# The last output stores of an attention and gated-unit kernel, on other issuing engines

## The chip, the cores and the metric

The kernel runs on one core of one Trainium2 chip. The metric is device time in microseconds. The kernel before takes 338.45 us, the median of 3 runs (337.93 to 338.51). The profiled execution took 338.22 us, of which the span from its first to its last instruction is 336.1 us.

Engines are named as in the profile: PE is TensorE (PEld its weight loads), DVE is VectorE, ACT is ScalarE, POOL is GpSimd, SP is SyncE. An engine name with a q behind it is that engine's queue of instructions that do no arithmetic: waits, drains, issues of transfers.

## The reference

Linear attention without a softmax, normalised per head, followed by a gated unit whose gate comes from a causal convolution over five tokens:

```python
# q, k, v: (8, 8, 576, 64) float32;  x: (8, 576, 512)
kv  = einsum('bhsd,bhse->bhde', k, v)
o   = einsum('bhsd,bhde->bhse', q, kv)
x   = (o / sqrt(mean(o * o, -1) + 1e-6) * g_norm)      # heads put side by side: (B, S, 512)
gate_pre = sum over k of conv_w[k] * x_padded[:, k:k + S, :]
gate = 1 / (1 + exp(-gate_pre))
out  = (gate * (x @ w_val)) @ w_out                     # (8, 576, 512) float32
```

The weights arrive as float64 and are narrowed on the chip. What matters here is only the last product and how its rows get to memory.

## The kernel before

The kernel works through eight batches. Two batches make a pair `i`; the output of a pair is stored in nine chunks of 128 tokens by 512 channels: chunks 0 to 7 from `fast_product`, two at a time, and chunk 8 with the 64 tokens that each of the two batches has left over. Chunk 8 of the last pair comes between its chunks 5 and 7 in time. A chunk is gathered in an SBUF tile `ot` (a ring of three buffers) and stored by four transfers of 32 rows each.

The seven products of a pair of chunks are made in PSUM by TensorE, and ScalarE and VectorE bring them together in the two chunks' halves (`LOW` is channels 0 to 255, `HIGH` the rest):

```python
    def fast_keep(i, p, n):
        # ... a, b, c: PSUM banks; first, second: the tiles of chunks 2p and 2p + 1
        if n == 0:
            nc.scalar.copy(out=first[:, LOW], in_=a)
        elif n == 1:
            nc.scalar.copy(out=second[:, HIGH], in_=c)
        elif n == 2:
            nc.scalar.copy(out=first[:, HIGH], in_=a)
        elif n == 3:
            add(first[:, LOW], b)          # VectorE
        elif n == 4:
            add(second[:, HIGH], a)        # VectorE
        elif n == 5:
            add(first[:, HIGH], c)         # VectorE: chunk 2p is complete
        else:
            nc.scalar.copy(out=second[:, LOW], in_=a)      # chunk 2p + 1 is complete
```

Chunk 8, and the store of any chunk (HB is 4, TB is 32):

```python
    def keep_out(i, c):
        ot = work.tile([P, C], FP32, tag="ot", bufs=3, name=f"ot{i}_{c}")
        nc.scalar.copy(out=ot[:], in_=st["po", i, c][:])
        st["ot", i, c] = ot

    def store(i, c, cols=slice(0, C), queues=(nc.sync,)):
        ot = st["ot", i, c]
        for j in range(HB):
            # ... bb, n: batch of the pair, and row block
            queues[j % len(queues)].dma_start(
                out=rows_out[2 * i + bb, n, :, cols], in_=ot[j * TB:(j + 1) * TB, cols])
```

All stores go out by SyncE, except those of the last two chunks, 6 and 7, of the last pair:

```python
    def last_stores(chunk, r, want):
        kept = lambda n: ("kept", (chunk[0], 3, n))
        if r == 0:                     # chunk 6: GpSimd, whole rows
            plan.add(
                "POOL", 2.4, want, store, *chunk, slice(0, C), (nc.gpsimd,), needs=[kept(3), kept(5)],
                frees=[("ot", chunk)], load=0.26 / RATE,
            )
            return
        plan.add(                      # chunk 7, upper half: SyncE
            "SP", 2.0, want, store, *chunk, HIGH, (nc.sync,), needs=[kept(4)], frees=[("ot", chunk)],
            load=0.13 / RATE,
        )
        plan.add(                      # chunk 7, lower half: SyncE and ScalarE in turn
            "SP", 1.0, want + 1.0, store, *chunk, LOW, (nc.sync, nc.scalar), needs=[kept(6)],
            frees=[("ot", chunk)], load=0.13 / RATE,
        )
```

`plan.add` hands a step to a planner that orders the steps of all engines by estimated start times; what it orders is then written out in that order. GpSimd's other work is a step of the normalisation, some copies, and the transfers `xT<-y` that move transposed blocks within SBUF (line 554). Every program ends with a closing block (line 1166 in the profile), in which SyncE waits for all transfers, every engine drains, and all engines meet twice at a barrier that GpSimd gathers and releases.

Of the kernel before, what the change touches and what calls it, by code (L numbers as in the profile page):

```python
# [136 lines left out]
def kernel(  # L137
# [37 lines left out]
    nc = tc.nc  # L175
    B, H, S, D = q.shape
    C = H * D
# [5 lines left out]
    TB = 32  # L183
# [21 lines left out]
    def ps(kind, shape, name):  # L205
        return psum.tile(shape, FP32, tag=kind, bufs=BANKS[kind], name=name)

    plan = Planner({
        "k0": 1, "k1": 1, "v0": 1, "v1": 1, "tails": 2, "q": 3, "w64": 3, "y": 2, "wexp": 2,
        "kv": 1, "kvbd": 2, "qT": 2, "tp": 1, "raw": 2, "mm": 4, "sq": 2, "ss": 3, "rt": 3,  # L210
        "x": 2, "xT": 2, "gate": GATES, "xs": 4, "gv": GVS, "ot": 3,
    }, by_batch=("tails", "kvbd", "xT", "gv"))
# [21 lines left out]
    LOW, HIGH = slice(0, C // 2), slice(C // 2, C)  # L234
# [129 lines left out]
    for jt in range(NK):  # L364
        cols = slice(jt * P, (jt + 1) * P)
# [290 lines left out]
    rows_out = out.rearrange("b (t n) c -> b n t c", n=NB)  # L656
# [86 lines left out]
        else:  # L743
            nc.scalar.copy(out=second[:, LOW], in_=a)

    def store(i, c, cols=slice(0, C), queues=(nc.sync,)):
        ot = st["ot", i, c]
        for j in range(HB):
            bb, n = divmod(c * HB + j, NJ * HB) if c < 2 * NJ else (j // 2, NJ * HB + j % 2)
            queues[j % len(queues)].dma_start(  # L750
                out=rows_out[2 * i + bb, n, :, cols], in_=ot[j * TB:(j + 1) * TB, cols])

    ORDER = [NJ] + list(range(NJ - 1, -1, -1))
    TAPS = range(K - 2, -1, -1)
    RATE = 0.27
# [204 lines left out]
    def single(b, first):  # L960

        key = b // 2, 2 * NJ
        plan.add(
            "PE", 3.6, first, out_product, *key,
            needs=gated_all(b - 1, b) + [("wout", jt) for jt in range(NK)],
            gives=[("po", key)], takes=[("mm", ("po", key))], frees=[("gv", b - 1), ("gv", b)],
        )
        plan.add(
            "ACT", 0.5, first + 3.6, keep_out, *key, needs=[("po", key)], gives=[("ot", key)],
            takes=[("ot", key)], frees=[("mm", ("po", key))],  # L970
        )
        plan.add(
            "SP", 2.0, first + 4.3, store, *key, needs=[("ot", key)], frees=[("ot", key)],
            load=0.26 / RATE,
        )

    def outputs(b, first):
# [9 lines left out]
        for m in range(2):  # L987
# [29 lines left out]
            for r, parts in enumerate(((3, 5), (4, 6))):  # L1017
                chunk = i, 2 * p + r
                if b == B - 1 and m:
                    last_stores(chunk, r, t + 6.8)  # L1020
                    continue
                plan.add(
                    "SP", 2.0, t + 6.8, store, *chunk, needs=[("kept", (i, p, n)) for n in parts],
                    frees=[("ot", chunk)], load=0.26 / RATE,
                )
# [2 lines left out]

    def last_stores(chunk, r, want):

        kept = lambda n: ("kept", (chunk[0], 3, n))
        if r == 0:
            plan.add(
                "POOL", 2.4, want, store, *chunk, slice(0, C), (nc.gpsimd,), needs=[kept(3), kept(5)],
                frees=[("ot", chunk)], load=0.26 / RATE,
            )
            return
        plan.add(
            "SP", 2.0, want, store, *chunk, HIGH, (nc.sync,), needs=[kept(4)], frees=[("ot", chunk)],
            load=0.13 / RATE,  # L1040
        )
        plan.add(
            "SP", 1.0, want + 1.0, store, *chunk, LOW, (nc.sync, nc.scalar), needs=[kept(6)],
            frees=[("ot", chunk)], load=0.13 / RATE,
        )

    def loads_kv(b, want):
# [62 lines left out]
    for n in range(4):  # L1110
        plan.add(
            "DVE", 0.61, begin + 20.0 + n, weight_sums, n,
            needs=[("wout", jt) for jt in range(NK)] + ([("wsum", n - 1)] if n else []), gives=[("wsum", n)],
        )
    for n in range(4):
        plan.add(
            "DVE", 0.61, 150.0 + n, val_sums, n,
            needs=[("wval", jt) for jt in range(NK)] + ([("vsum", n - 1)] if n else []), gives=[("vsum", n)],
# [52 lines left out]
```

## Time and profile before

| | |
|---|---|
| time, median of 3 runs | 338.45 us (337.93 to 338.51) |
| span of the profiled execution | 336.1 us |
| mean granted TensorE clock | 0.981 |
| PE busy | 315.5 us, 94% |
| DVE busy | 279.0 us, 83% |
| ACT busy | 150.5 us, 45% |
| POOL busy | 139.5 us, 41% |
| output stores by SyncE, 64 KB / 32 KB | 136 / 6 |
| output stores by GpSimd, 64 KB | 4 |
| output stores by ScalarE, 32 KB | 2 |

Busy times are read with care. They are averages over the whole span; a change at the very end of the program is judged by what ends last there. The time given for an issue of a transfer is that of the engine handing it over, and not of the data's way; the profile gives the time from issue to landing separately. Times in the text are counted from the first instruction of the span.

### The profile page before, as it was taken

What the parts mean: (1) busy time and instruction counts of PE and PEld (TensorE: products, weight loads), DVE (VectorE), ACT (ScalarE), POOL (GpSimd) and SP (SyncE); (2) the same over time, 40 slices, a digit from 0 to 9 for tenths busy, and PEclk for the clock granted to TensorE, in tenths of its full rate; (3) what the DMA queues carried; (4) which work ended last, traced back from release to release, by engine and by line L of the source; (5) the groups of instructions that cost most, each with busy time, mean ns of one, the idle gap of its engine ahead of it and who ended that gap; (6) DMA issues with size and microseconds to landing.
All of it is one profiled execution on the core that took longest, in us unless ns stands there. A gap on an engine that the chain in (4) does not pass through costs nothing.

```text
span 336.1 us, 6353 instructions
## 1 busy us (share of the span) xinstructions
PE 315.5 (94%) x2221; PEld 253.6 (75%) x2221; DVE 279.0 (83%) x504; ACT 150.5 (45%) x325; POOL 139.5 (41%) x182
## 2 busy tenths in 40 slices
PE   5599999999999999999999999999999999999970
PEld 4589878878878688878876878788786678887820
DVE  1628889999999999998989989988999999997210
ACT  1649769583253445242453434425454244353210
POOL 3006523534467659676003328866344670000020
PEclk9599999999999999999999999999999999999996
DMA  6999979792698689899749568225400333122230
GB/s 206 317 250 350 269 193 336 183 291 72 162 250 244 169 236 264 204 237 263 208 101 304 151 181 245 41 53 146 96 0 1 96 64 77 49 62 54 68 87 11
DMA packets 46142, 55.36 MB, mean 165 GB/s; under 512 B 15819, under 2 KB 36575, under 8 KB 46111
## 3 DMA queue, kind: packets, MB, share of 16 engines
q1 hardware_dynamic: 42654, 48.34, 52.7%
q0 software_dynamic: 3200, 6.56, 8.5%
q8 instruction: 17, 0.28, 0.4%
q14 instruction: 15, 0.11, 0.1%
q10 hardware_dynamic: 256, 0.07, 0.1%
HBM read 39.21 MB, written 9.44 MB: 145 GB/s over the span
## 4 chain that ended last, share of the span: by engine, by line
PE 87%; DMA 4%; DVE 3%; SPq 1%; ACT 1%; issue 1%; POOL 0%; POOLq 0%; DVEq 0%
PE val L583 19%; PE a L721 15%; PE cb L721 12%; PE raw L485 10%; PE va L633 9%; PE kv L408 6%; PE vc L633 4%; PE out L664 4%; DMA q<-in_q_dram 3%; PE qTps L446 3%; PE vb L633 2%; PE kv L397 2%; PE xTps L531 2%; DVE gate L571 1%; DMA vl<-in_v_dram 1%
## 5 line engine op out<-in xcount | busy, mean ns | idle before, releaser
L513 POOL TENSOR_TENSOR rt<-ss,mhalf 128x8 f32<-128x8 f32 (+1 forms) x40 | 68.0, 1706 | 117.3 <-DVE ss L507 117.2
L571 DVE SCALAR_TENSOR_TENSOR gate<-xT,cwT,gate 128x576 f32<-128x576 f32 x128 | 98.7, 809 | 1.7 <-ACT gate L565 1.6
L583 PE MATMUL val<-xT,wval 128*128 128x288 f32 x256 | 66.3, 408 | 0.0
L554 POOL DMA_DIRECT2D xT<-y x96 | 52.9, 557 | 14.6 <-DVE ss L507 4.7
L583 PEld LDWEIGHTS val<-xT,wval 128*128 128x128 f32 x256 | 47.5, 190 | 11.8
L485 PEld LDWEIGHTS raw<-kvbd,qT 128*128 128x128 f32 (+1 forms) x320 | 35.3, 180 | 6.5 <-issue 4.3
L485 PE MATMUL raw<-kvbd,qT 128*128 128x128 f32 (+1 forms) x320 | 39.1, 280 | 0.3 <-ACT kvbd L418 0.3
L499 ACT ACTIVATE sq<-raw 128x512 f32<-128x512 f32 (+1 forms) x40 | 22.1, 553 | 27.3 <-PE raw L485 26.3
L721 PE MATMUL a<-wsum,sums 128*128 128x256 f32 x128 | 33.3, 382 | 0.7 <-ACT ot L732 0.6
L730 DVE TENSOR_TENSOR ot<-cb,ot 128x256 f32<-128x256 f32 x32 | 13.4, 420 | 19.1 <-PE cb L721 10.4
L592 ACT COPY gv<-val 128x288 f32<-128x288 f32 x32 | 12.7, 397 | 35.3 <-PE val L583 35.1
L721 PEld LDWEIGHTS a<-wsum,sums 128*128 128x128 f32 x128 | 23.7, 190 | 5.1 <-ACT ot L732 1.3
L507 DVE TENSOR_REDUCE ss<-sq 128x8 f32<-128x520 f32 (+1 forms) x40 | 25.0, 625 | 2.1 <-ACT sq L499 2.0
L596 DVE TENSOR_TENSOR gv<-gv,gate 128x576 f32<-128x576 f32 x32 | 23.5, 747 | 3.1 <-ACT gate L578 1.3
L521 DVE TENSOR_TENSOR x<-raw,rt 128x512 f32<-128x512 f32 (+1 forms) x40 | 24.9, 625 | 0.6 <-POOL rt L513 0.5
L565 ACT ACTIVATE gate<-xT,cwT 128x576 f32<-128x576 f32 x32 | 23.4, 769 | 3.0 <-DVE gv L596 2.7
L578 ACT ACTIVATE gate<-gate 128x576 f32<-128x576 f32 x32 | 21.4, 682 | 5.9 <-DVE gate L571 5.3
L750 POOL DMA_DIRECT2D out_dram<-ot x4 | 2.0, 503 | 50.3 <-DVE ot L730 50.3
L408 PEld LDWEIGHTS kv<-v,k 128*64 128x64 f32 x512 | 17.6, 137 | 4.4 <-issue 3.5
L408 PE MATMUL kv<-v,k 128*64 128x64 f32 x512 | 20.5, 225 | 0.0
L633 PE MATMUL va<-xs,vsum 128*128 128x288 f32 x64 | 18.1, 406 | 0.0
L721 PE MATMUL cb<-wsum,sums 128*128 128x256 f32 x64 | 16.8, 386 | 0.3 <-DVE sums L697 0.3
(107 smaller groups left out, 521.8 us busy)
## 6 DMA issues: line engine op xcount, KB each, us to landing
q<-in_q_dram SPq DMA_DIRECT2D x96, 140.0 KB, 5.0
out_dram<-ot SPq DMA_DIRECT2D x136, 64.0 KB, 1.8
k<-in_k_dram SPq DMA_DIRECT2D x16, 512.0 KB, 6.4
v<-in_v_dram SPq DMA_DIRECT2D x16, 512.0 KB, 5.4
xT<-y POOLq DMA_DIRECT2D x96, 64.0 KB, 2.9
w_wval<-in_moe_w_val_dram SPq DMA_DIRECT2D x4, 512.0 KB, 7.2
q<-in_q_dram SPq DMA_DIRECT2D x4, 512.0 KB, 8.7
w_wout<-in_moe_w_out_dram SPq DMA_DIRECT2D x4, 512.0 KB, 8.3
```

The source lines that it names most:

```text
L408: nc.tensor.matmul(kvp[r * D:(r + 1) * D, hp, :], st["k", b, half][:, h, j, :] if j < NJ else kl[:, 2 * hp + r, :], st["v", b, half][:, h, ...
L485: nc.tensor.matmul(raw[row * m:(row + 1) * m, col * P:(col + 1) * P], st["qT", b][:, hp, c * P:c * P + m], kv_bd[b % 2][:, hp, :], start=T ...
L507: nc.vector.reduce_sum(out=ss[:, 0:n], in_=st["sq", b, c][:, 0:n], axis=AX.X)
L513: nc.gpsimd.tensor_tensor(out=rt[:, 0:n], in0=st["ss", b, c][:, 0:n], in1=mhalf[:, 0:n], op=ALU.pow)
L521: nc.vector.tensor_tensor(out=x[:, 0:n * D].rearrange("p (h e) -> p h e", h=n), in0=st["raw", b, c][:, 0:n * D].rearrange("p (h e) -> p h ...
L554: nc.gpsimd.dma_start(out=xTs[b % 2][i * TB:(i + 1) * TB, :, first:first + P], in_=y[a * TB:(a + 1) * TB, i])
L565: nc.scalar.activation(out=gate[:], in_=xTs[b % 2][:, jt, HALO:SX], func=AF.Copy, scale=cwT[:, K - 1, jt:jt + 1])
L571: nc.vector.scalar_tensor_tensor(out=gate[:], in0=xTs[b % 2][:, jt, tap * TB:tap * TB + S], scalar=cwT[:, tap, jt:jt + 1], in1=gate[:], op ...
L583: nc.tensor.matmul(val[:], wval[:, kc, jt * P:(jt + 1) * P], xTs[b % 2][:, kc, HALO + n * SV:HALO + (n + 1) * SV], start=(kc == 0), stop=( ...
L596: nc.vector.tensor_tensor(out=both, in0=both, in1=st["gate", b, jt][:], op=ALU.mult)
L633: nc.tensor.matmul(st[bank, "val", b, mj][:], weights_[:, k], tokens()[:, k], start=(n in (0, 1, 3) and k == 0), stop=(k == NK // 2 - 1), ...
L721: nc.tensor.matmul(st[bank, i, p], tokens()[:, k], weights_[:, k], start=(n < 2 and k == 0), stop=(k == NK // 2 - 1), skip_group_check=True)
```

## The change

In the last pair, chunk 6 is stored by SyncE instead of GpSimd, and chunk 7 by ScalarE alone, in whole rows, instead of in halves by SyncE and ScalarE. GpSimd then issues no store. It is meant to leave all stores to SyncE and ScalarE, to keep rows whole (2,048 bytes instead of 1,024), and to free GpSimd at the end.

```diff
-    def store(i, c, cols=slice(0, C), queues=(nc.sync,)):
+    def store(i, c, queue=nc.sync):
         ot = st["ot", i, c]
         for j in range(HB):
             bb, n = divmod(c * HB + j, NJ * HB) if c < 2 * NJ else (j // 2, NJ * HB + j % 2)
-            queues[j % len(queues)].dma_start(
-                out=rows_out[2 * i + bb, n, :, cols], in_=ot[j * TB:(j + 1) * TB, cols])
+            queue.dma_start(out=rows_out[2 * i + bb, n], in_=ot[j * TB:(j + 1) * TB, :])
@@
     def last_stores(chunk, r, want):
-        kept = lambda n: ("kept", (chunk[0], 3, n))
-        if r == 0:
-            plan.add(
-                "POOL", 2.4, want, store, *chunk, slice(0, C), (nc.gpsimd,), needs=[kept(3), kept(5)],
-                frees=[("ot", chunk)], load=0.26 / RATE,
-            )
-            return
-        plan.add(
-            "SP", 2.0, want, store, *chunk, HIGH, (nc.sync,), needs=[kept(4)], frees=[("ot", chunk)],
-            load=0.13 / RATE,
-        )
         plan.add(
-            "SP", 1.0, want + 1.0, store, *chunk, LOW, (nc.sync, nc.scalar), needs=[kept(6)],
-            frees=[("ot", chunk)], load=0.13 / RATE,
+            "ACT" if r else "SP", 1.8, want, store, *chunk, nc.scalar if r else nc.sync,
+            needs=[("kept", (chunk[0], 3, n)) for n in ((3, 5), (4, 6))[r]], frees=[("ot", chunk)],
+            load=0.26 / RATE,
         )
```

On each engine the other instructions stand in the same order. On SyncE the four stores of chunk 8 are followed by the four of chunk 6; on ScalarE the last copy of chunk 7 is followed by its four stores.

## The prediction

> **What bounds the kernel now.** I read the page first (TensorE busy for 94% of a span of 336.1 us), then the chain of waits in the last stretch, then the table by stretches, then the instructions of the closing block, engine by engine. The chain says that work ends near 327 us. From the window 320 to 337 us:
> ```profile
> 7 pieces in order of time: start us, us, what
> ...
> 323.27 1.07 PE cb L721 x4
> 324.35 0.02 issue
> 324.37 0.44 DVE ot L730
> 324.81 0.28 issue
> 325.09 1.50 POOL out_dram L750 x3
> 326.59 0.49 POOLq L1166
> ```
> The last thing the chain names is GpSimd's store of chunk 6, and then GpSimd's own closing instruction, at 327.08 us. The span ends at 336.1. So nine microseconds follow in which nothing computes, and the table by stretches shows that nothing is transferred in them either (columns: stretch, its length, busy time of PE, PEld, DVE, ACT and POOL, TensorE clock, DMA share, GB/s):
> ```profile
> 325.00:327.00 2.00, 0.20 (x1) 0.00 (x0) 0.00 (x0) 0.37 (x1) 1.91 (x4) 1.00 0.64 172
> 327.00:329.00 2.00, 0.00 (x0) 0.00 (x0) 0.00 (x0) 0.00 (x0) 0.08 (x1) 1.00 0.42 129
> 329.00:336.00 7.00, 0.00 (x0) 0.00 (x0) 0.00 (x0) 0.00 (x0) 0.00 (x0) 0.58 0.00 0
> ```
> The closing block is line 1166, where the tile context ends. Its instructions on GpSimd, and then on SyncE between 326.6 and 335 us (durations in ns: least, median, most; then first and last start in us):
> ```profile
> L1166 POOLq EVENT_SEMAPHORE  x4: 17/17/17, 335.4 to 336.0; - x4
> L1166 POOLq DRAIN  x3: 34/102/8913, 326.4 to 335.8; - x3
> ```
> ```profile
> L1166 SPq EVENT_SEMAPHORE  x9: 27/28/61, 326.7 to 329.1; - x9
> L1166 SPq DRAIN  x2: 7/7/7, 329.1 to 329.2; - x2
> ```
> One of GpSimd's three drains takes 8,913 ns. It starts at 326.4, behind its four stores, and so ends at 335.32; GpSimd's first closing semaphore follows at 335.4 and the span ends 0.77 us after the drain (336.09 - 335.32). SyncE, which waits for every store to land, is through at 329.2 and then has nothing to do until 335.5. So in the last stretch GpSimd's drain ends last, by 6.1 us (335.3 - 329.2). It isn't the landing of the data: from 329 us the DMA share is 0.00. And GpSimd would have been free long before, because the waits charge its first store with 50.3 us of idle time:
> ```profile
> L750 POOL DMA_DIRECT2D out_dram<-ot x4 | 2.0, 503 | 50.3 <-DVE ot L730 50.3
> ```
> Its last other work is eight transfers xT<-y, 270.49 to 274.83 us in the timeline.
>
> **What the skill says.** VectorE: DVE Perf Modes, "The DRAIN you can't avoid", speaks of boilerplate drains of about 12 ns on all engines in preamble and postamble. SyncE's 7 ns agree; GpSimd's 8,913 ns do not, and the measurement decides. No page says what a GpSimd drain waits for. DMA: Bandwidth & Descriptors, "Anatomy of one DMA", gives a GpSimd transfer about 2.0 us fixed plus bytes over 436 GB/s, for 64 KB an estimate of 2.15 us; this trace has 2.2 us for GpSimd's stores and 1.6 to 2.1 for SyncE's 64 KB ones. The same page, "Issuing engines are not separate DMA queues", says that all issuers share 16 engines and that a second issuer saves only issue time; here landings stretch from 1.6 us (SyncE alone, 323.98) to 2.4 us (326.20, three issuers at once), so I give the new stores about 2 us while both queues run.
>
> **The change, part by part.** *Removed:* GpSimd's four stores, 4 x 503 ns of issue beside other work. With them goes the reason for GpSimd to stand at the end: its program then ends with the xT<-y transfers at 274.8, the drain starts there and, even at 9 us and some landing, is over before 290. Worth up to the 6.1 us above; what is left of it depends on when the last store lands.
> *Moved to SyncE:* chunk 6, four stores of 64 KB after chunk 8's four, in place of two half-row stores of chunk 7. *Moved to ScalarE:* all of chunk 7, four whole-row stores, in place of two of half rows; the upper half, stored at 320.24 before, now also waits for ScalarE's last copy. *Same:* everything on TensorE and VectorE, and ScalarE up to that copy; the built program has the same order there. So the last copy still ends at 325.60 (325.23 + 0.37).
>
> ScalarE: issues at 325.66 and then every 0.40 to 0.47 us (its two were 0.40 apart, SyncE's 0.47); the fourth at about 326.98 lands near 329.0.
>
> SyncE: chunk 8 as before, 323.98, 324.33, 324.80, 325.27, done at 325.69. Chunk 6 has been ready since 324.80. But the built program shows a new wait. Stores on the two hardware queues take eight semaphores in turn, and each store first waits until the last one with the same semaphore has landed. The program's last stores on SyncE and ScalarE, with waits:
> ```
> SP  L750 DMACopy out<-ot_6 32x512 [waits DMAHW4, DVE]
> SP  L750 DMACopy out<-ot_6 32x512 [waits DMAHW6]
> SP  L750 DMACopy out<-ot_6 32x512 [waits DMAHW7]
> SP  L750 DMACopy out<-ot_6 32x512 [waits DMAHW0]
> ACT L750 DMACopy out<-ot_7 32x512 [waits DVE, ACT]     raises DMAHW7
> ```
> DMAHW7 belongs to ScalarE's first store of chunk 7. So chunk 6's first two stores go at 325.73 and 326.20 (DMAHW6's owner, issued 324.33, landed after 1.7), but its third waits until ScalarE's first has landed: 325.66 + 2.0 = 327.66, so about 327.7. The fourth goes at 328.15 and lands, with the queues emptying, 1.8 us later: 329.95. That is 0.95 us after ScalarE's last.
>
> Closing: in the trace SyncE passes the newest landing at 328.6 and needs until 329.2 for the other seven waits and two drains, 0.6 us; the newest one is second in that list again. 329.95 + 0.6 = 330.55. Then 0.05 for the signal to GpSimd, and from GpSimd's semaphore at 335.36 to the end 0.73 us: 331.3. The span goes from 336.1 to 331.3, 4.8 us less, and the time from 338.45 to 333.65, that is 1.4% faster.
>
> **Rivals.** *The drain is a fixed cost of the end:* if it takes its 8.9 us whenever the kernel closes, or waits there for something else than GpSimd's own stores, nothing is gained: 338.4. For it: this trace has just one long drain, and it does not end with the last landing but 6.5 us later. Against: it has no semaphore wait in the program and it started at 326.4 as soon as GpSimd reached it, while SyncE was still waiting; and GpSimd's drain at the very start of the kernel, before any of its transfers, took 0.18 us. One in twenty.
> *No hold on the semaphore matters:* if ScalarE's first store lands sooner, or SyncE's third is not held, ScalarE's fourth sets the end at 329.0; its wait is the seventh of nine in SyncE's list, so some 0.25 us of it remain, 329.0 + 0.25 + 0.05 + 0.73 = 330.0, and the time is 338.45 - 6.1 = 332.35. For it: half rows landed in 1.5 us when alone (321.5 us). Against: 1.9 us for ScalarE's own store at 325.64.
> *Whole rows collide:* twelve stores of 64 KB, 786 KB, in 324 to 328.6 us. If landings grow to 2.4 us as the last one did before, the third goes at 328.1, the fourth lands at 330.8, and the time is 334.5. Against: from 324 us on the kernel before moved 655 KB (eight of 64 KB, four of 32 KB), with 0.64 and 0.42 of the DMA engines' time taken.
> *TensorE takes the bound:* it is busy for 94%, and after the change it still is; it ends at 325.20 before and after, so it fixes the floor of all this, not the gain.
>
> **Range and chances.** Centre 333.6. The sum's weak terms are two landings in series (0.3 us either way for each) and the runs' own spread (337.93 to 338.51). 332.6 to 334.6 should hold it 8 times in 10; the rest lies mostly above, where the drain stays. Faster by over 2% needs 331.68, a span that ends at 329.3, just 0.3 us after ScalarE's fourth store lands by my sum, with 0.78 us of closing still to come: 0.03. Slower by over 2% has no mechanism here: 0.01. Within 2%: 0.96.
>
> **What would show it.** Right: in the closing block GpSimd's long drain starts near 275 us and no GpSimd instruction but semaphores and short drains stands after 327; SyncE's drain comes within 1 us of the end; SyncE's four chunk-6 stores show a gap of about 1 us before the third, with a landing of ScalarE's store as releaser. Wrong: a drain of some 9 us that still starts after 326 us (first rival), or four chunk-6 stores without a gap (second). A TensorE end other than 325.2 us would mean that something upstream moved, which nothing in the program's order suggests.

## The result, and the profile after

The changed kernel takes 333.64 us (median of 4 runs, 333.30 to 334.14), the kernel before beside it 338.48 us: a ratio of 0.9856, 95% interval 0.9832 to 0.9880. In a later comparison of the same two kernels it was 333.05 against 338.61 us, 0.9844 (0.9828 to 0.9860). The change makes the kernel about 1.5% faster.

The closing block of the changed kernel (its line is 1155 now), GpSimd's instructions, with durations in ns (least, median, most) and first and last start in us:

```profile
L1155 POOLq EVENT_SEMAPHORE  x4: 17/17/17, 330.9 to 331.5; - x4
L1155 POOLq DRAIN  x3: 34/102/10560, 273.0 to 331.3; - x3
```

The long drain is still there. It now starts at 273.0 and ends at 283.6, in the shade of 40 us of TensorE's work, and not at 335.3. The table by stretches shows that the dead time of 7 us without work or transfers is gone:

```profile
325.00:327.00 2.00, 1.05 (x5) 0.57 (x3) 0.42 (x1) 0.37 (x1) 0.00 (x0) 1.00 0.39 98
327.00:329.00 2.00, 0.00 (x0) 0.00 (x0) 0.00 (x0) 0.00 (x0) 0.00 (x0) 0.93 0.86 221
329.00:331.60 2.60, 0.00 (x0) 0.00 (x0) 0.00 (x0) 0.00 (x0) 0.00 (x0) 0.50 0.21 57
```

The chain of waits in the window 323 to 332 us now ends with ScalarE's last copy, and what follows is issue, landing and barrier:

```profile
5 pieces in order of time: start us, us, what
...
325.18 0.88 PE a L721 x4
326.06 0.02 issue
326.08 0.37 ACT ot L744
```

SyncE's own waits from 323 to 332 us hold the two that the new end consists of, 0.7 us before its third store of chunk 6 and 1.2 us for the last landing:

```profile
SPq L1155 <- DMA out_dram<-ot: 1.2, 1, 1.2
SPq L750 <- DMA out_dram<-ot: 0.7, 1, 0.7
```

For everything below I use the tail: the time from the end of TensorE's last product to the end of the span. It leaves out what happens at the start of a run. Before it was 336.09 - 325.20 = 10.9 us, after it is 331.58 - 326.05 = 5.5 us. A second profile of the changed kernel gives 5.5 us again (330.92 - 325.38; 5.54 and 5.53), while whole runs of the kernel before differ by up to 1.7 us.

### The profile page after: what moved, and what is told of

It is laid out like the page before. It is cut to its first block, busy times and chain, and to the rows that moved or that the text cites. A ratio compares the mean times of both kernels' runs of the same rounds, so it can differ in the third digit from the quotient of the medians.

```text
span 331.6 us, 6348 instructions
## 1 busy us (share of the span) xinstructions
PE 316.0 (95%) x2221; PEld 254.1 (77%) x2221; DVE 279.1 (84%) x504; ACT 150.5 (45%) x325; POOL 137.1 (41%) x178
## 4 chain that ended last, share of the span: by engine, by line
PE 88%; DVE 4%; DMA 3%; ACT 1%; issue 1%; SPq 1%; DVEq 0%
PE val L583 19%; PE a L721 15%; PE cb L721 12%; PE raw L485 10%; PE va L633 9%; PE kv L408 6%; PE vc L633 4%; PE out L664 4%; DMA q<-in_q_dram 3%; PE qTps L446 3%; PE vb L633 2%; PE kv L397 2%; PE xTps L531 2%; DVE gate L571 1%; DVE gv L596 1%
## 5 line engine op out<-in xcount | busy, mean ns | idle before, releaser
L721 PE MATMUL a<-wsum,gv 128*128 128x256 f32 x64 | 16.8, 386 | 0.1
```

Source lines behind the costliest of these rows:

```text
L721: nc.tensor.matmul(st[bank, i, p], tokens()[:, k], weights_[:, k], start=(n < 2 and k == 0), stop=(k == NK // 2 - 1), skip_group_check=True)
```

## The experiments

**One store by GpSimd.** Only the first row block of chunk 6 goes back to GpSimd.

```diff
-            queue.dma_start(out=rows_out[2 * i + bb, n], ...)
+            by = nc.gpsimd if (i, c, j) == (B // 2 - 1, 6, 0) else queue
+            by.dma_start(out=rows_out[2 * i + bb, n], ...)
```

> The changed kernel, but GpSimd stores the first of chunk 6's four row blocks (one transfer of 64 KB), SyncE the other three. Theory (the drain is a price for any transfer that GpSimd has issued shortly before it closes, nearly whatever the number): a long drain of 7 to 9 us starts near 326 us and the time is 337.0 to 338.5, all of the gain lost to one transfer. Rival (the drain's length goes with the number of transfers issued since the last quiet time, four before): about a quarter, 2 to 3 us, hidden behind the other stores, time 333.0 to 333.7.

336.87 us (7 runs), just under the expected 337.0 to 338.5, ratio 0.9944 (0.9924 to 0.9963), tail 9.2 us. GpSimd's store and its closing drain:

```profile
L751 POOL DMA_DIRECT2D out_dram<-ot x1: 518/518/518, 324.5 to 324.5; - x1
```

```profile
L1156 POOLq DRAIN  x3: 34/102/8538, 324.5 to 333.5; - x3
```

One transfer brings back an 8.5 us drain, so the rival (a quarter of it) falls. That two thirds of the tail's gain are lost (3.6 of 5.4 us) and not all of it follows from the issue: GpSimd is done 0.4 us after TensorE's end (325.00 against 324.59) and not 1.9 us after it (327.08 against 325.20), as it is with four stores.

**A copy by GpSimd, no store.** After VectorE has completed chunk 6, GpSimd copies one column of it into an unused constant.

```diff
+    def touch(i, c):
+        nc.gpsimd.tensor_copy(mhalf[:, 0:1], st["ot", i, c][:, 0:1])
```

> The changed kernel, and GpSimd copies one column of chunk 6's tile into an unused constant after VectorE has completed it; it issues no transfer at the end. GpSimd so reaches its closing drain at about 326 us, as in the kernel before, with its last transfers more than 50 us back. Theory (the drain's length comes from GpSimd's transfers of just before): the drain is short, under 1 us, and the time stays at 333.0 to 334.2. Rival (GpSimd's closing drain takes its 9 to 10 us whenever it is reached, for instance because it tidies up after all 96 transfers of the run): the drain ends near 335 to 336 us and the time is 337.5 to 339.5. The rival would say that what counts is the time at which GpSimd is done, with whatever work, and not the kind of work.

333.32 us, ratio 0.9851 (0.9825 to 0.9876), tail 5.6 us. The time is what my theory said, but the drain is not:

```profile
L1039 POOL COPY mhalf<-ot x1: 187/187/187, 319.8 to 319.8; 128x1 f32<-128x1 f32 x1
```

```profile
L1160 POOLq DRAIN  x3: 34/102/8132, 319.8 to 330.8; - x3
```

With its last transfer 45 us back, GpSimd's drain takes 8.1 us all the same. My theory, that the transfers of just before make it long, is refuted. The time stayed because I had placed the copy badly: column 0 lies in the lower half of the chunk, complete before 319.8 us, so the drain was over at 327.9, ahead of the last landing.

Set side by side, the drains so far have one more regularity. Counted from the end of GpSimd's last instruction they last 7.92 us where GpSimd had issued 96 transfers in the whole run (7.94 in this run), 8.00 with 97, and 8.24 with 100. That is 82 ns for each transfer of the run. The next three experiments are made from this.

**The copy placed right.** The column copied is the first of the upper half.

```diff
-        nc.gpsimd.tensor_copy(mhalf[:, 0:1], st["ot", i, c][:, 0:1])
+        nc.gpsimd.tensor_copy(mhalf[:, 0:1], st["ot", i, c][:, C // 2:C // 2 + 1])
```

> As the run with a late copy on GpSimd, but the column copied lies in the upper half of chunk 6, which VectorE completes last; GpSimd so gets its copy at about 325.6 and not at 319.8 us. No transfer by GpSimd within 50 us. Theory now (the closing drain takes 82 ns for each transfer that GpSimd has issued in the whole run, counted from the end of GpSimd's last instruction; 96 of them, 7.9 us): the drain ends near 333.9, the span at 334.7, the time is 336.4 to 337.2. Rival (the drain needs GpSimd's transfers to be recent, and the 8.1 us of the run before had another cause): time 333.0 to 333.9.

336.62 us, ratio 0.9936 (0.9913 to 0.9959), span 334.4, tail 8.6 us.

```profile
L1160 POOLq DRAIN  x3: 34/102/8133, 325.5 to 334.1; - x3
```

A copy of 188 ns that nobody needs, without any transfer, costs 3.1 us of tail. So GpSimd's stores were not expensive as stores. What costs is that GpSimd, after its 96 transfers, has anything to do late.

**No transfers by GpSimd at all, and half of them.** With the same late copy, SyncE issues all transfers xT<-y, or those of batches 2 to 4. The order of SyncE's loads changes with it, so only the drain is read here; the times, 351.67 and 359.33 us in one run each, say nothing of the end.

```diff
-            nc.gpsimd.dma_start(
+            nc.sync.dma_start(                               # no transfers
+            (nc.sync if b < 5 else nc.gpsimd).dma_start(     # half of them
```

> As the run before, but all 96 transfers xT<-y are issued by SyncE, so that GpSimd issues no transfer in the whole run; only the length of GpSimd's closing drain is read, not the time, since SyncE's loads now stand behind these transfers. Theory (82 ns per transfer of the run): the drain is under 0.3 us. Rival (a fixed closing cost of GpSimd of 8 us, whatever it has done): 7.5 to 8.5 us.

> As the run before, but the transfers of batches 2, 3 and 4 are issued by SyncE and those of batches 5, 6 and 7 by GpSimd: 48 by GpSimd instead of 96. Read is the length of GpSimd's closing drain. Theory (82 ns per transfer of the run): 3.9 to 4.1 us after its last copy. Rival (one price as soon as GpSimd has issued any transfer): 7.5 to 8.5 us.

The closing drains, of the kernel without transfers by GpSimd and of the one with 48:

```profile
L1160 POOLq DRAIN  x3: 34/78/263, 344.4 to 349.4; - x3
```

```profile
L1160 POOLq DRAIN  x3: 34/102/4213, 351.0 to 357.0; - x3
```

From the end of the copy: 0.07 and 4.01 us. Both are within what the count of transfers said, and the fixed price is refuted twice.

| transfers by GpSimd in the run | kernel | drain after GpSimd's last instruction |
|---|---|---|
| 0 | late copy, none by GpSimd | 0.07 us |
| 48 | late copy, half by GpSimd | 4.01 us |
| 96 | changed kernel; late copy | 7.92; 7.94 us |
| 97 | one store | 8.00 us |
| 100 | kernel before; early stores | 8.24; 8.24 us |

**Twice as many, of half the size.** Each of the 96 transfers is issued as two.

```diff
-            nc.gpsimd.dma_start(out=xTs[b % 2][..., :, first:first + P], in_=y[..., i])
+            for two in (EVEN, ODD):
+                nc.gpsimd.dma_start(out=xTs[b % 2][..., two, first:first + P], in_=y[..., i, two])
```

> As the run with the copy at 325.6 us, but each of GpSimd's 96 transfers is issued as two of half the size: 192 transfers, the same bytes. Read is the length of GpSimd's closing drain after its last copy, not the time, since issuing takes GpSimd longer. Theory (82 ns per transfer issued): 15.5 to 16.1 us. Rival (the price goes with the bytes moved, or with the data packets if these stay the same in number): 7.7 to 8.2 us.

```profile
L1161 POOLq DRAIN  x3: 34/102/6090, 334.5 to 341.1; - x3
```

5.9 us after the copy, which is neither. All transfers up to there had 64 KB, and their number, their bytes and their packets (32 each) went up together. With 192 transfers of 32 KB, the same bytes and twice the packets, the drain comes to 31 ns for each transfer, and to less than before for the same bytes. So "82 ns per transfer" holds for up to 100 transfers of 64 KB and not as a law of the number alone. Whether size counts, or whether something is settled during the run once there are more than some number, these runs do not tell.

**Stores by GpSimd, but early.** GpSimd stores chunk 4 of the last pair.

```diff
+                early = (b, m, r) == (B - 1, 0, 0)
                 plan.add(
-                    "SP", 2.0, t + 6.8, store, *chunk, ...
+                    "POOL" if early else "SP", 2.0, t + 6.8, store, *chunk, nc.gpsimd if early else nc.sync, ...
```

> The changed kernel, but GpSimd stores chunk 4 of the last pair (four transfers of 64 KB, about 10 us before the end), SyncE no longer does. Theory (only a drain that is reached late costs time): the drain starts near 317 us, lasts 8 to 10 us and is over by 327, before the last store has landed; time 333.0 to 334.2. Rival (stores by GpSimd cost the same wherever they stand in the last stretch, say because their slower landing holds the ring of three tiles): 335 or more.

333.29 us, ratio 0.9848 (0.9820 to 0.9875), tail 5.3 us.

```profile
L1157 POOLq DRAIN  x3: 34/102/8915, 317.4 to 331.3; - x3
```

As many stores of the same size and the same 8.9 us drain as in the kernel before, but over at 326.3. They cost nothing here. The position decides.

**Either half of the change alone.** First chunk 6 by SyncE, with chunk 7 as before; then chunk 7 whole by ScalarE, with chunk 6 by GpSimd as before.

```diff
-                "POOL", 2.4, want, store, *chunk, slice(0, C), (nc.gpsimd,), needs=[kept(3), kept(5)],
+                "SP", 2.4, want, store, *chunk, slice(0, C), (nc.sync,), needs=[kept(3), kept(5)],
```

```diff
-            "SP", 2.0, want, store, *chunk, HIGH, (nc.sync,), needs=[kept(4)], ...
-            "SP", 1.0, want + 1.0, store, *chunk, LOW, (nc.sync, nc.scalar), needs=[kept(6)], ...
+            "ACT", 1.8, want, store, *chunk, slice(0, C), (nc.scalar,), needs=[kept(4), kept(6)], ...
```

> The kernel before, but with chunk 6 stored by SyncE instead of GpSimd; chunk 7 stays in halves, the upper one stored early by SyncE, the lower one by SyncE and ScalarE in turn. Theory (all of the gain is that GpSimd is done early; whole rows for chunk 7 bring nothing): SyncE has ten stores to issue at the end and lands the last one at about the same time as in the changed kernel, 333.0 to 334.2. Rival (whole rows by ScalarE alone carry part of the gain): 334.5 or more.

> The kernel before, but with chunk 7 stored whole by ScalarE; GpSimd stores chunk 6 as before. Theory (GpSimd's drain after 100 transfers sets the end, 8.24 us after its last store): 338.0 to 339.0, no change. Rival (halves by two queues cost something of their own at the end): 337.5 or less.

| | chunk 7 in halves | chunk 7 whole, by ScalarE |
|---|---|---|
| chunk 6 by GpSimd | 338.61 us, tail 10.9 | 338.42 us, tail 10.9; ratio 0.9997 (0.9985 to 1.0009) |
| chunk 6 by SyncE | 333.67 us, tail 5.5; ratio 0.9851 (0.9824 to 0.9877) | 333.05 and 333.64 us, tail 5.5 |

All of the gain is chunk 6 leaving GpSimd. Whole rows for chunk 7 bring nothing: with GpSimd at the end they are hidden behind the drain, and without it SyncE is through 4.8 us after TensorE's end in both versions. With chunk 7 in halves its last store goes 0.4 us later (2.9 us after TensorE's end, being the tenth, against 2.5 us with the wait), but the closing waits behind the last landing then take 0.3 us and not 0.6.

**Seven stores by SyncE, five by ScalarE.** The last row block of chunk 6 goes out by ScalarE, in the last 0.4 us of its wait for TensorE's last product.

```diff
-            "ACT" if r else "SP", 1.8, want, store, *chunk, ...          # all four row blocks
+            part("SP", range(HB - 1), want)                              # chunk 6, blocks 0 to 2
+            part("ACT", range(HB - 1, HB), want + 20.0)                  # chunk 6, block 3
+            part("ACT", range(HB), want)                                 # chunk 7
```

> The changed kernel, but the last row block of chunk 6 goes out by ScalarE, ahead of its last copy, so that SyncE issues seven of the last twelve stores and ScalarE five. No store of SyncE then waits for the landing of one of ScalarE. Theory (SyncE's wait for the semaphore of ScalarE's first store, 0.7 us, stands on the path to the end): the last issues are near 327.9 us, the last landing is ScalarE's at 329.7 instead of SyncE's 330.24, and it is last in SyncE's list of closing waits; 0.8 to 1.1 us faster than the changed kernel, 332.5 to 332.9. Rival (the two queues are limited by the landing itself, and the wait only stands in place of a queue of data): less than 0.3 us faster, 333.3 to 333.7; or slower, if ScalarE's early store delays its last copy.

> The changed kernel again, beside the version with seven stores by SyncE and five by ScalarE, on one chip: 333.0 to 333.8, ratio to the kernel before 0.984 to 0.987.

> Seven stores by SyncE, five by ScalarE, again. Theory (SyncE's wait for ScalarE's first landing stands on the path): 0.5 to 1.0 us under the changed kernel of the same call. Rival (the first difference was the start of the kernel, which moves the whole run by up to 0.9 us): within 0.3 us of it.

332.62 us, ratio 0.9823 (0.9791 to 0.9856), and in the second comparison 332.69 us, 0.9833 (0.9816 to 0.9851), beside 333.05 us for the changed kernel. SyncE's waits in the same stretch as above, of this kernel's first run:

```profile
SPq L750 <- ACT ot L672: 5.1, 1, 5.1
SPq L1160 <- DMA out_dram<-ot: 1.4, 1, 1.4
```

The wait of 0.7 us ahead of a store is gone, and the tail is 4.76 us (4.78 in the second run) against 5.54 and 5.53: 0.77 us less, about what a wait of 0.7 us on the path would give. The medians do not show it evenly: 1.0 us between the first runs and 0.4 us in the second comparison, where I had expected 0.5 at least, and the intervals of the two versions overlap. What differs is the start of the runs (below), and each run's mean granted TensorE clock (a share of full speed) tells the starts apart. At 0.980 to 0.982 the changed kernel took 333.72 and 334.14 us and this version 332.96 to 333.06 (four runs); at 0.988 to 0.990, 333.05 against 332.04 and 332.20; at 0.995 and above, 332.78 to 333.56 (six runs) against 332.39 and 332.42. The means of each group differ by 0.8 to 0.9 us, though these are few runs, sorted afterwards. The experiment takes away the wait and moves one issue at once, so how much either does was not separated. The version has the lowest medians of those run; that it is over 2% faster than the kernel before is not shown.

## Why the prediction was right

333.6 us was predicted, and 333.64 measured. By its own steps:

*What ends last, and what the change removes.* Right. The drain was the last thing in the kernel before, and now it starts at 273.0 us, where 274.8 was expected: its record begins while GpSimd still issues its last transfers (until 275.7), which is 2.6 us of its 10.6. It is over 47 us before SyncE is through. The first rival's outcome, nothing gained, did not happen. But part of its premise is true: most of the drain does not come from GpSimd's four stores. Without them 7.9 of 8.2 us are still to be paid, only earlier. With one small errand left late on GpSimd (the late copy) the tail was 8.6 us, and over half of the gain was gone.

*Why the drain is so long.* The prediction left this open. One of its arguments against the first rival was the short drain at the start of the kernel, 0.18 us. That fits what the runs found, a price for the transfers issued up to then. My first guess after the result, recent transfers, was wrong. The comparison with the Trainium skill was loose: VectorE: DVE Perf Modes, "The DRAIN you can't avoid", gives about 12 ns on all engines for the boilerplate drains of preamble and postamble, while the drains here carry a line of the kernel's own program, its closing block. SyncE's takes 7 ns; GpSimd's ends 0.07 us after its last copy without a transfer in the run and 7.9 us after it with 96.

*SyncE's wait for ScalarE's first landing.* Right in mechanism, a little too long in size. SyncE's stores in the changed kernel between 324 and 329.5 us:

```profile
L750 SPq DMA_DIRECT2D out_dram<-ot x8: 314/420/438, 324.8 to 328.5; - x8
L750 SPq EVENT_SEMAPHORE  x1: 17/17/17, 326.6 to 326.6; - x1
...
DMA to landing us min/median/max: 1.7/1.7/2.1
```

ScalarE's first store went at 326.49 and landed at 328.15, after 1.66 us, where I had taken 2.0; SyncE's third followed at 328.17, and the fourth 0.36 us later (I had 0.45). It landed after 1.7 us instead of 1.8, and SyncE was through at 330.8. The terms of the closing, 0.6 and 0.73 us, were measured as 0.56 and 0.73. In sum the tail is 5.5 us where the steps gave 331.3 - 325.2 = 6.1; the landing of ScalarE's first store is over half of the difference.

*TensorE's end at 325.2 us.* Missed, in the other direction. In the profiled run it is 326.05. Everything on TensorE is late by 0.8 us from 17.5 us on, with the same program up to there. The table by stretches, kernel before and then after:

```profile
10.00:20.00 10.00, 7.84 (x91) 7.57 (x93) 6.72 (x16) 7.12 (x18) 0.00 (x0) 0.69 1.19 266
16.00:17.00 1.00, 1.00 (x10) 0.88 (x11) 1.00 (x3) 0.00 (x0) 0.00 (x0) 0.92 1.22 280
17.00:18.00 1.00, 1.00 (x20) 1.00 (x22) 0.93 (x3) 0.00 (x0) 0.00 (x0) 1.00 1.39 174
```

```profile
10.00:20.00 10.00, 7.96 (x77) 7.58 (x79) 6.72 (x16) 6.39 (x15) 0.00 (x0) 0.59 1.18 271
16.00:17.00 1.00, 1.00 (x7) 1.00 (x6) 1.00 (x3) 0.00 (x0) 0.00 (x0) 0.50 1.23 268
17.00:18.00 1.00, 1.00 (x9) 0.78 (x10) 0.93 (x3) 0.00 (x0) 0.00 (x0) 0.50 1.42 173
```

The granted clock (third number from the right) is back at full by 17 us in the kernel before and still at half until 18 us in the changed one, and the two stretches from 16 to 18 us hold 30 matmuls there and 16 here (one of line 397 takes 275 ns there and 421 ns here). The change cannot reach there. The same split runs through the profiles of kernels that differ only at the end: in seven of them the clock between 17 and 18 us is 0.50 to 0.52, and TensorE ends at 325.8 to 326.5 us; in three it is 1.00, and TensorE ends at 324.6 to 325.4 us. (An eleventh has no clock on record before 17 us.) Why the clock comes back earlier in some runs stays open. So the hit to within 0.1 us owes something to two misses that cancel. The tail says the change is worth 5.4 us, and the prediction said 4.8; the medians of the two comparisons gave 4.8 and 5.6.

*The second rival*, no wait for the semaphore, was wrong: the wait was there, 0.7 us. *Colliding whole rows* was wrong too: the stores at the end landed in 1.7 to 2.1 us, where the kernel before had up to 2.4 with three issuers. *The chances:* what was given 0.96 came about, the ratio's interval, 0.9832 to 0.9880, lies wholly within 2%.

## What to carry to other kernels

Look past the last useful instruction: the time between it and the end of the span belongs to the kernel too, and an engine with little to do may own it. If GpSimd has issued transfers anywhere in a run, let it finish early, since here it needed 8 us to close after 96 of them, and the smallest late errand (one column copied, one store) puts these on the path. When transfers share semaphores in turn across two queues, look at which transfer each one waits for; one more on the other queue took that wait away.

## What the runs showed of the hardware

GpSimd's closing drain took 0.07 us plus 82 ns for each 64 KB transfer that GpSimd had issued since the start of the run (0, 48, 96, 97 and 100 transfers), counted from the end of GpSimd's last instruction, even with the last transfer 50 us back. With 192 transfers of 32 KB it took 5.9 us, which no simple count explains; this stays open.

The granted TensorE clock was 0.50 for some us within the first 20 us of the run. This was over at 15.6 to 16.2 us in three profiles and at 18.0 to 19.0 us in seven, of kernels with the same program up to there. TensorE's work ended at 324.6 to 325.4 us in the three and at 325.8 to 326.5 us in the seven.
